# Sums of w_out 192 bytes further into their buffers, and the MLP's pool 192 bytes further

## The chip, the cores and the metric

The kernel runs on 1 core of one Trainium2 chip. The metric is the device time of one execution in microseconds (us); the kernel before takes 634.56 us, the median of 3 runs (634.4 to 636.4). Lower is better.

## The reference

Three layers follow one another on 8 batches of 576 rows, 4608 rows in all, in fp32.

```python
def _attn_ref(q, k, v, p):            # q, k, v [8, 8, 576, 64]; p [8, 8, 32, 64]
    p_packed = sm_attn(p, k, v)       # 32 packed rows per head attend over 576 keys
    return sm_attn(q, p_packed, p_packed)

def _moe_ref(x, phi, w1, w2):         # x [4608, 512], 8 experts of 4 slots, F 1024
    logits = x @ phi                  # [4608, 32]
    d = softmax(logits, axis=0); slot_input = d.T @ x        # [32, 512]
    slot_out[e] = np.maximum(slot_input[e] @ w1[e], 0.0) @ w2[e]
    c = softmax(logits, axis=1); return c @ slot_out          # [4608, 512]

def _moe2_ref(x, w_in, w_out):        # w_in [512, 2048], w_out [2048, 512]
    h = x @ w_in
    g = h * np.tanh(softplus(h))      # Mish
    return g @ w_out                  # [4608, 512]
```

## The kernel before, in words

The first two layers take the first 230 us or so. The rest is the third layer, the MLP, and only this part is touched. Since `c @ slot_out @ w_in` has rank 32, `slot_out @ w_in` is formed once (the tile MS), and the product with the combine weights (CS) gives `h` directly: four matmuls of 256 columns per step (L1205, `emit_h`). ScalarE applies Mish (L1210). The 4608 rows are cut into 18 blocks `n` of 256, the 2048 hidden features into 4 chunks `c` of 512. A step is one (n, c): it multiplies a 256 x 512 piece of g with a 512 x 512 piece of w_out and adds it into PSUM banks that hold the block's output.

To keep fp32 accuracy with one-pass matmuls of type fp32r, each operand is split into a high part that is exact in fp32r and a low rest: gh and gl (ScalarE casts, VectorE subtracts, `emit_c`), and whi and wlo for w_out. Each product is then three matmuls: high by high, high by low, low by high.

There are two kinds of steps. A plain step (the first blocks) multiplies with moving operands of 512 columns straight from whi and wlo (the tile W3, shown as W). A fast step (`fast`, 59 of 72) uses a scheme of Strassen's kind: the 2 x 2 blocks of g and of w_out are combined into sums, and 7 products of half size replace 8. The sums of g are S, with its parts Sh and Sl (k = 0 to 3; `emit_m`, `emit_c`), made anew in every step. The sums of w_out are T1, T2, T3 for each of the 4 chunks, made once in `build_t` and then only read. The order of the products of a fast step is in `emit_o`: Z (gh by W), V (S1 by T2), W (S2 by T3), X or W (S3 by W), U (S0 by T1), Y and X (gh by W). Each product is 6 matmuls of 256 columns (1024 bytes per partition): 4 with the high weights, 2 with the low ones. With two `h` matmuls after Z and two after the product into the bank W a fast step has 46 matmuls; in the last two steps, which have no `h` to prepare, 42. In the first fast step of a block the first matmul on bank W is 512 columns wide (`TT["open"]`) and clears both halves.

In a matmul g, S or MS is the stationary operand (weights, loaded before each matmul), W, T or CS the moving one. Where they lie in SBUF, in bytes from the start of a partition:

| buffer | role | address before | modulo 512 |
|---|---|---|---|
| whi, wlo (W3) | moving | 115712 + 2048 i, halves of 1024 | 0 |
| CS | moving (`h`) | 189440 + 1024 n | 0 |
| T, 7 buffers of ring_a | moving | 18240 + 4608 i, and + 1024 z f | 320 |
| T, 4 buffers of ring_x | moving | 66880 + 4608 i, and + 1024 z f | 320 |
| T, one in pool g2 (i == 11) | moving | 109888, and + 1024 z f | 320 |
| gh, gl (pool wg) | weights | 50496 + 4096 i, and + 512 f | 320 |
| S, Sh, Sl (pool g2) | weights (Sh, Sl) | 85312, 93504, 101696, two buffers of 4096 each | 320 |
| MS | weights (`h`) | 181248 + 512 m | 0 |

The pool g2 is opened when the pools of the conversion (t2, tp) are closed, at step N0, and lies where they lay. The order of all instructions is written by hand. TensorE runs through the steps without a gap as long as the sums and casts of the next step come in time; VectorE makes them and also empties the PSUM banks (`emit_store`, L1376).

Of the kernel before, what the change touches and what calls it, by code (L numbers as in the profile page):

```python
# [9 lines left out]
F32 = mybir.dt.float32  # L10
F32R = mybir.dt.float32r
# [8 lines left out]
def kernel(  # L20
# [1124 lines left out]
    def msb_c(n, copy, mp, i=0, w=512):  # L1145
        copy(out=msb[n][:, i:i + w], in_=mp[:, 0:w])

    def emit_mr(n, mr, i=0, w=512):
        nc.tensor.matmul(mr[:, 0:w], lhsT=idrep, rhs=msb[n][:, i:i + w], start=True, stop=True)

    def ms_c(n, mr, i=0, w=512):
        nc.scalar.copy(out=MS[:, 512 * n + i:512 * n + i + w], in_=mr[:, 0:w])

    def ms_l(n, mr, i=0, w=512):
        dst = MS[64:128, 512 * n + i:512 * n + i + w]
        nc.vector.tensor_tensor(out=dst, in0=mr[64:128, 0:w], in1=dst.bitcast(F32), op=ALU.subtract)
# [14 lines left out]
    def fast(n, c):  # L1171

        return not PLAIN.get(n, 0) >> c & 1
# [23 lines left out]
    def emit_h(n, c, z):  # L1197

        if not z:
            s = tp.tile([128, 1024], F32, name="s", tag="s") if steps.index((n, c)) < N0 else two_of("s")  # L1200
            blk["m", n, c] = s.rearrange("p (f n) -> p f n", f=4), None
        hp = ps_b.tile([128, 512], F32, name="h3", tag="h3", bufs=2)
        for f in range(2):
            ft = 4 * c + 2 * z + f
            nc.tensor.matmul(  # L1205
                hp[:, 256 * f:256 * f + 256], lhsT=MS[:, 128 * ft:128 * ft + 128], rhs=CS[:, 256 * n:256 * n + 256],
                start=True, stop=True,
            )
        s = blk["m", n, c][0][:, 2 * z:2 * z + 2]
        nc.scalar.activation(out=s, in_=hp.rearrange("p (f n) -> p f n", f=2), func=AF.Mish)  # L1210
# [36 lines left out]
    def wparts(c):  # L1247
        return whi[:, 4 * c:4 * c + 4], wlo[:, 4 * c:4 * c + 4]

    def build_t(c, ws=None):  # L1250

        H, L = wparts(c)
        TT[c] = []

        def alloc():
            for k in range(3):
                i = (3 * c + k + 9) % 12
                if i < 7:
                    t = ring_a.tile([128, 18 * D], F32, name="T", tag="ring%d" % (5, 6, 2, 0, 1, 4, 3)[i])
                elif i < 11:  # L1260
                    t = ring_x.tile([128, 18 * D], F32, name="T", tag=("kT", "qT")[i % 2])
                else:
                    t = g2.tile([128, 1280], F32, name="T", bufs=1)
                    TT["open"] = t.bitcast(F32R)[:, 256:1280].rearrange("p (z n) -> p z n", z=4)[:, 0:4:3]
                    nc.gpsimd.tensor_scalar_mul(
                        out=t[:, 1024:1280].bitcast(F32R).rearrange("p (z n) -> p z n", z=2),
                        in0=ident[:, None, :].to_broadcast([128, 2, 128]), scalar1=0.0,
                    )
                t = t[:, 0:1024].bitcast(F32R).rearrange("p (z f n) -> p z f n", z=2, f=2)
                TT[c].append((t[:, 0], t[:, 1]))  # L1270
            TT[c].append((H[:, 0:2, 256:512], L[:, 0:2, 256:512]))

        if c != 1:
            alloc()
        minus = lambda o, x, y: nc.vector.tensor_tensor(out=o, in0=x, in1=y, op=ALU.subtract)
        if ws is None:
            wa, wb = (w[:, 0:1024].rearrange("p (f n) -> p f n", f=2) for w in (held if c == 1 else (two_of("osb"), two_of("osb"))))
            B11, B12, B21, B22 = (w[:, :, 256 * j:256 * j + 256] for w in (wa, wb) for j in range(2))
            T4 = B21
            if c != 1:  # L1280
                for w, f in ((wa, 0), (wb, 2)):
                    nc.vector.tensor_tensor(out=w, in0=H[:, f:f + 2].bitcast(F32), in1=L[:, f:f + 2].bitcast(F32), op=ALU.add)
                yield
            minus(B11, B12, B11)
            minus(B12, B22, B12)
            minus(B22, B22, B11)
            minus(B21, B21, B22)
            T = B11, B22, B12
            yield
            if c == 1:  # L1290
                alloc()
            for (hi, lo), x in zip(TT[c], T):
                nc.scalar.copy(out=hi, in_=x)
            for (hi, lo), x in zip(TT[c], T):
                minus(lo, x, hi.bitcast(F32))
        else:
            T4 = AY[:, 4096:4608].rearrange("p (f n) -> p f n", f=2)
            for f in range(2):
                (B11, B12), (B21, B22) = ((w[:, 0:256], w[:, 256:512]) for w in (ws[f], ws[2 + f]))
                minus(B11, B12, B11)  # L1300
                minus(B12, B22, B12)
                minus(B22, B22, B11)
                minus(T4[:, f], B21, B22)
            yield
            fx = [(f, hi, lo, x) for f in range(2) for (hi, lo), x in zip(TT[c], (ws[f][:, 0:256], ws[2 + f][:, 256:512], ws[f][:, 256:512]))]
            for f, hi, lo, x in fx:
                nc.scalar.copy(out=hi[:, f], in_=x)
            for f, hi, lo, x in fx:
                minus(lo[:, f], x, hi[:, f].bitcast(F32))
        yield  # L1310
        hi, lo = TT[c][3]
        nc.scalar.copy(out=hi, in_=T4)
        minus(lo, T4, hi.bitcast(F32))
        yield
# [54 lines left out]
    def quads(n):  # L1369
        if ("q", n) not in blk:  # L1370
            osb = two_of("osb").rearrange("p (z n) -> p z n", z=2)
            blk["q", n] = [osb] + [osb[:, i, 256 * j:256 * j + 256] for i in range(2) for j in range(2)]
        return blk["q", n]
# [36 lines left out]
    def bank(x):  # L1410
        if x in "xs":
            return ps_x.tile([128, 512], F32, name="o3", tag="x") if x == "x" else ps_so.tile([128, 512], F32, name="so")
        return ps_b.tile([128, 512], F32, name="o3", tag=x, bufs=2 if x == "h3" else 1)
# [25 lines left out]
    def two_of(x):  # L1439

        turn[x] ^= 1
        i = (0 if x == "osb" else 2048) + 1024 * turn[x]
        return AY[:, i:i + 1024]
# [40 lines left out]
    for i, (n, c) in enumerate(steps):  # L1484
        if i == 2:
            R.update(X=bank("X2"), Y=bank("Y2"))
        if i == N0:
            wp.close()
            g2 = ctx.enter_context(tc.tile_pool(name="g2", bufs=2, reuse_waits="tile"))
        if i == N0 + 2:  # L1490
            R.update(Z=R["X0"], V=R["Y0"], W=R["X1"], U=R["Y1"])
        nx = steps[i + 2] if i + 2 < len(steps) else None
        last_s = fast(n, c) and c == ORDER[n][-1]

        def mid(z):
            if z == 0 and last_s:
                nc.scalar.copy(out=quads(n)[1], in_=rq("Z"))
            if z == 1 and last_s:
                add(quads(n)[2], quads(n)[1], rq("V"))
            if z in (0, 2) and nx:  # L1500
                emit_h(*nx, z // 2)
                if i == 0:
                    m = 2 + z // 2
                    blk["mr", m] = bank("XY"[z // 2] + "2")
                    emit_mr(m, blk["mr", m])

        if i + 1 < len(steps):
            emit_c(*steps[i + 1])
        if i == 0:
            msb_c(2, nc.scalar.copy, mp2)  # L1510
            msb_c(3, nc.scalar.copy, mp3)
            ms_c(1, mr1)
            ms_l(1, mr1)
        if i < N0:
            cvt(CVT[i][0])
        emit_o(n, c, mid)
        if i == 0:
            cvt("u4 m4")
            for m in (2, 3):
                ms_c(m, blk["mr", m])  # L1520
                ms_l(m, blk["mr", m])
        early = c == ORDER[n][-1] and n + 1 in PLAIN and not fast(n + 1, ORDER[n + 1][0])
        if early and last_s:
            emit_store(n)
        if nx:
            emit_m(*nx)
        if i < N0:
            cvt(CVT[i][1])
        if i == N0 - 1:
            work[3] = build_t(3, [late_w[k][3] for k in range(12, 16)])  # L1530
        if c == ORDER[n][-1] and not (early and last_s):
            emit_store(n)
        for x in TW.get(i, ""):
            next(work[int(x)])
# [31 lines left out]
```

## Time and profile before

| | |
|---|---|
| time, median of 3 runs | 634.56 us (634.4 to 636.4) |
| profiled execution, its own time | 633.09 us |
| span of the profiled execution | 631.3 us |
| TensorE busy | 603.5 us, 96%, 5874 matmuls |
| VectorE busy | 499.5 us, 79% |
| ScalarE busy | 339.4 us, 54% |
| granted TensorE clock | full in all 40 slices |
| fast steps | 59, from about 290 us to the end |

A matmul's record begins when it is handed on and ends when its last column is out; several are under way at once. So busy time says little about the rate: what a matmul costs in a run of matmuls is the distance from one start to the next. Where the timeline merges matmuls into one row (x4, x2), the distance is the difference of the starts of two rows divided by the matmuls between them. Starts are printed to 0.01 us, so a distance over 12 matmuls is good to about 1 ns, one over 2 matmuls to about 5 ns.

### The profile page before, as it was taken

The page shows a single profiled execution, that of the slowest core. Times are in us where ns is not written, and L with a number is a line of the kernel's source. Part 1 is how long each engine was busy: PE and PEld are TensorE (multiplying, and loading weights), DVE is VectorE, ACT ScalarE, POOL GpSimd, SP SyncE. Part 2 cuts the span into 40 slices and gives each one's busy share as a digit, 9 for nine tenths or more (in the row PEclk, how much of TensorE's full clock was granted, in tenths as well). Part 3 has the DMA queues.
Part 4 walks back from the last instruction along what each step waited for, and adds up shares of the span by engine and source line. Part 5 has one row for each costly group of instructions (what it writes and reads, how often), then busy time and mean ns, then how long its engine had stood idle before and what let it go on. Part 6 is the DMA issues. An engine that isn't in the chain of part 4 may idle for free.

```text
span 631.3 us, 14397 instructions
## 1 busy us (share of the span) xinstructions
PE 603.5 (96%) x5874; PEld 522.3 (83%) x5874; DVE 499.5 (79%) x1004; ACT 339.4 (54%) x684; POOL 47.3 (7%) x73
## 2 busy tenths in 40 slices
PE   7799999998998999999999999999999999999997
PEld 4577777786434468888989999999999999999997
DVE  4998888978464388988999887788778877887883
ACT  3354555546334486665556555555555555555551
POOL 5122222112030000000000000000000000000000
PEclk9999999999999999999999999999999999999999
DMA  8998963999999962002110110011011101110100
GB/s 274 329 323 293 330 210 128 404 412 407 394 410 413 413 243 67 2 0 68 35 35 0 35 35 12 24 34 34 2 34 34 34 2 34 34 34 2 34 34 35
DMA packets 42162, 89.61 MB, mean 142 GB/s; under 512 B 10736, under 2 KB 19056, under 8 KB 42096
## 3 DMA queue, kind: packets, MB, share of 16 engines
q1 hardware_dynamic: 41696, 88.36, 39.2%
q8 instruction: 46, 0.75, 0.5%
q10 hardware_dynamic: 144, 0.26, 0.1%
q14 instruction: 20, 0.16, 0.1%
q0 software_dynamic: 256, 0.07, 0.1%
HBM read 79.23 MB, written 9.44 MB: 140 GB/s over the span
## 4 chain that ended last, share of the span: by engine, by line
PE 65%; DVE 19%; DMA 8%; ACT 5%; issue 2%; SPq 1%; DVEq 0%; POOL 0%; ACTq 0%; POOLq 0%
PE o L1327 44%; PE so L1327 7%; DMA AW<-in_moe_w_dram 6%; PE h L1205 5%; DVE kT L338 4%; DVE S L1221 2%; DVE A L510 1%; DVE AY L1376 1%; DVE mx L509 1%; PE s L490 1%; DVE Sl L1240 1%; DVE sm L525 1%; DMA AW<-in_q_dram 1%; DVE nmx L386 1%; DMA AC<-in_k_dram 1%
## 5 line engine op out<-in xcount | busy, mean ns | idle before, releaser
L1327 PE MATMUL o<-W,gh 128*128 128x256 f32 (+1 forms) x648 | 119.2, 311 | 0.5 <-DVE AY L1376 0.5
L1327 PE MATMUL o<-T,Sh 128*128 128x256 f32 x708 | 114.8, 284 | 1.0 <-DVE AY L1376 0.9
L1236 ACT CAST gh<-AY 128x512 fp32r<-128x512 f32 x118 | 54.7, 511 | 113.5 <-PE o L1327 113.5
L1327 PEld LDWEIGHTS o<-W,gh 128*128 128x128 f32 x648 | 95.6, 188 | 7.9 <-issue 1.3
L1327 PEld LDWEIGHTS o<-T,Sh 128*128 128x128 f32 x708 | 97.0, 189 | 2.1 <-issue 0.6
L1210 ACT ACTIVATE AY<-h 128x512 f32<-128x512 f32 x126 | 74.0, 594 | 26.3 <-PE h L1205 25.0
L1239 DVE TENSOR_TENSOR gl<-AY,gh 128x512 fp32r<-128x512 f32 x118 | 60.4, 553 | 33.3 <-ACT gh L1236 33.3
L1240 DVE TENSOR_TENSOR Sl<-S,Sh 128x1024 fp32r<-128x1024 f32 x59 | 72.1, 1223 | 9.2 <-ACT Sh L1237 9.2
L1327 PE MATMUL o<-T,Sl 128*128 128x256 f32 x354 | 71.2, 282 | 0.0
L1327 PE MATMUL o<-W,gl 128*128 128x256 f32 (+1 forms) x324 | 70.0, 308 | 0.0
L1237 ACT CAST Sh<-S 128x1024 fp32r<-128x1024 f32 x59 | 61.9, 1049 | 6.8 <-DVE S L1221 6.8
L1205 PE MATMUL h<-CS,W 128*128 128x256 f32 x288 | 56.2, 284 | 0.0
L1327 PEld LDWEIGHTS o<-W,gl 128*128 128x128 f32 x324 | 52.1, 188 | 4.0
L1327 PEld LDWEIGHTS o<-T,Sl 128*128 128x128 f32 x354 | 54.8, 190 | 0.0
L1221 DVE TENSOR_TENSOR S<-AY 128x256 f32<-128x256 f32 x118 | 49.6, 420 | 6.0 <-ACT AY L1210 6.0
L1376 DVE TENSOR_TENSOR AY<-AY,o 128x256 f32<-128x256 f32 x115 | 45.1, 417 | 9.1 <-PE o L1327 5.3
L1205 PEld LDWEIGHTS h<-CS,W 128*128 128x128 f32 x288 | 44.1, 188 | 3.1 <-ACT s L1210 0.8
L1327 PE MATMUL so<-W,gh 128*128 128x256 f32 (+1 forms) x268 | 45.4, 292 | 0.0
L1327 PEld LDWEIGHTS so<-W,gh 128*128 128x128 f32 x268 | 37.3, 188 | 2.4 <-ACT W L1191 0.3
L376 PE MATMUL s<-kT,win 128*128 128x288 f32 x128 | 34.7, 414 | 4.7 <-ACT win L388 3.8
L1327 PE MATMUL o<-W,Sh 128*128 128x256 f32 x236 | 37.5, 281 | 0.0
L490 PE MATMUL s<-win,qT 128*128 128x128 f32 x256 | 32.1, 278 | 1.8 <-ACT win L356 1.8
(263 smaller groups left out, 988.9 us busy)
## 6 DMA issues: line engine op xcount, KB each, us to landing
AW<-in_moe_w_dram SPq DMA_DIRECT2D x45, 512.0 KB, 10.1
r_wo<-in_moe_w_out_dram SPq DMA_DIRECT2D x16, 512.0 KB, 8.9
out_dram<-AY SPq DMA_DIRECT2D x64, 128.0 KB, 2.1
r_wi<-in_moe_w_in_dram SPq DMA_DIRECT2D x13, 512.0 KB, 10.5
AW<-in_q_dram SPq DMA_DIRECT2D x11, 576.0 KB, 5.3
AW<-in_k_dram SPq DMA_DIRECT2D x9, 576.0 KB, 7.3
AW<-in_v_dram SPq DMA_DIRECT2D x40, 128.0 KB, 5.0
AC<-in_moe_w_dram SPq DMA_DIRECT2D x10, 512.0 KB, 10.0
```

What stands on the lines that cost most here:

```text
L338: nc.vector.transpose(out=T[:, dh, main].rearrange("p (i r a) -> p a i r" if nm == "k" else "p (i a r) -> p a i r", i=4, a=4,), in_=x[:, 0 ...
L376: nc.tensor.matmul(ps[:, n, 0:288], lhsT=pBD[b % 2][:, hq, dh], rhs=kT[:, dh, 288 * n:288 * n + 288], start=(dh == 0), stop=(dh == 1),)
L490: nc.tensor.matmul(ps[:, k - lo], lhsT=d["qT", hq][:, dh, 64 + 128 * i:192 + 128 * i], rhs=ppBD[b % 2][:, hq, dh], start=(dh == 0), stop=( ...
L1205: nc.tensor.matmul(hp[:, 256 * f:256 * f + 256], lhsT=MS[:, 128 * ft:128 * ft + 128], rhs=CS[:, 256 * n:256 * n + 256], start=True, stop=True,
L1210: nc.scalar.activation(out=s, in_=hp.rearrange("p (f n) -> p f n", f=2), func=AF.Mish)
L1221: nc.vector.tensor_tensor(out=S[:, k], in0=x, in1=y, op=op)
L1236: nc.scalar.copy(out=gh[:, f, t], in_=s[:, f, t])
L1237: nc.scalar.copy(out=Sh, in_=S)
L1239: nc.vector.tensor_tensor(out=gl[:, f, t], in0=s[:, f, t], in1=gh[:, f, t].bitcast(F32), op=ALU.subtract)
L1240: nc.vector.tensor_tensor(out=Sl, in0=S, in1=Sh.bitcast(F32), op=ALU.subtract)
L1327: nc.tensor.matmul(o, lhsT=lhsT, rhs=rhs, start=first, stop=stop)
L1376: add = lambda o, x, y: nc.vector.tensor_tensor(out=o, in0=x, in1=y, op=ALU.add)
```

## The change

Each sum T of w_out begins 48 elements (192 bytes) further into its buffer of 4608 bytes; it takes 4096 of them, so it fits. The one T that lies in pool g2 keeps its place in its tile, but in g2 an unused tile of 192 bytes is allocated first, which moves everything in that pool by 192 bytes: S, Sh, Sl and that T.

```diff
@@ build_t, alloc @@
-                t = t[:, 0:1024].bitcast(F32R).rearrange("p (z f n) -> p z f n", z=2, f=2)
+                o = 0 if i == 11 else 48
+                t = t[:, o:o + 1024].bitcast(F32R).rearrange("p (z f n) -> p z f n", z=2, f=2)
@@ the loop over steps @@
         if i == N0:
             wp.close()
             g2 = ctx.enter_context(tc.tile_pool(name="g2", bufs=2, reuse_waits="tile"))
+            g2.tile([128, 48], F32, name="pad", bufs=1)
```

After it T begins at 0 modulo 512, and so do the weights Sh and Sl; gh and gl stay at 320. All instructions are the same, in the same order on every engine. One wait is new: the first S of the program now overlaps a buffer of the conversion pool that VectorE read last, so its first instruction waits for VectorE's own earlier work too. On VectorE, before (the names are the program's: S the sums of g, gl the low part of g, w a converted block of w_out):

```order
439 L1275 TENSOR_TENSOR T<-w_3413,T 128x256 [waits Activation_49]
440 L1275 TENSOR_TENSOR T<-w_3363,T 128x256 [waits Activation_49]
441 L1230 TENSOR_TENSOR gl<-AY,gh 128x1024 [waits PE_49,Activation_49]
442 L1221 TENSOR_TENSOR S<-AY 128x256 [waits Activation_49]
443 L1221 TENSOR_TENSOR S<-S,AY 128x256 [waits DVE_49]
```

And after, at the same place:

```order
439 L1276 TENSOR_TENSOR T<-w_3413,T 128x256 [waits Activation_49]
440 L1276 TENSOR_TENSOR T<-w_3363,T 128x256 [waits Activation_49]
441 L1230 TENSOR_TENSOR gl<-AY,gh 128x1024 [waits PE_49,Activation_49]
442 L1221 TENSOR_TENSOR S<-AY 128x256 [waits DVE_49,Activation_49]
443 L1221 TENSOR_TENSOR S<-S,AY 128x256 [waits DVE_49]
```

Nothing moved; the fourth row has the second wait.

## Rows read from the trace of the kernel before

**Rows 1.** The page's parts 1 and 2: engines, then 40 slices of the span.
```profile
PE 603.5 (96%) x5874; PEld 522.3 (83%) x5874; DVE 499.5 (79%) x1004; ACT 339.4 (54%) x684; POOL 47.3 (7%) x73
...
PEclk9999999999999999999999999999999999999999
```

**Rows 2.** The page's part 4: chain that ended last, by engine, then by line.
```profile
PE 65%; DVE 19%; DMA 8%; ACT 5%; issue 2%; SPq 1%; DVEq 0%; POOL 0%; ACTq 0%; POOLq 0%
PE o L1327 44%; PE so L1327 7%; DMA AW<-in_moe_w_dram 6%; PE h L1205 5%; DVE kT L338 4%; DVE S L1221 2%; DVE A L510 1%; DVE AY L1376 1%; DVE mx L509 1%; PE s L490 1%; DVE Sl L1240 1%; DVE sm L525 1%; DMA AW<-in_q_dram 1%; DVE nmx L386 1%; DMA AC<-in_k_dram 1%
```

**Rows 3.** Waits of TensorE, 312 to 631 us (total us, times, longest us).
```profile
PE o L1327 <- DVE AY L1376: 1.1, 3, 0.4
```

**Rows 4.** Timeline of TensorE, end of the last but one step, last step (start, length).
```profile
621.27 0.62 PE L1327 MATMUL o<-W,gh 128*128 128x256 f32 x4
...
622.63 0.63 PE L1327 MATMUL o<-T,Sh 128*128 128x256 f32 x4
...
623.34 0.64 PE L1327 MATMUL o<-T,Sh 128*128 128x256 f32 x4
623.81 0.40 PE L1327 MATMUL o<-T,Sl 128*128 128x256 f32 x2
624.05 0.64 PE L1327 MATMUL o<-W,Sh 128*128 128x256 f32 x4
624.52 0.39 PE L1327 MATMUL o<-W,Sl 128*128 128x256 f32 x2
624.75 0.63 PE L1327 MATMUL o<-T,Sh 128*128 128x256 f32 x4
...
625.46 0.63 PE L1327 MATMUL o<-W,gh 128*128 128x256 f32 x4
```

**Rows 5.** Timeline of TensorE in plain steps, 512 columns wide.
```profile
242.34 0.62 PE L1205 MATMUL h<-CS,W 128*128 128x256 f32 x4
242.81 2.03 PE L1327 MATMUL o<-W,gh 128*128 128x512 f32 x8
...
245.60 2.03 PE L1327 MATMUL so<-W,gh 128*128 128x512 f32 x8
...
248.40 0.62 PE L1205 MATMUL h<-CS,W 128*128 128x256 f32 x4
```

**Rows 6.** Timeline of one whole fast step, 481.92 to 487.31 us, TensorE's and VectorE's rows.
```profile
481.92 0.62 PE L1327 MATMUL so<-W,gh 128*128 128x256 f32 x4
...
482.60 0.40 PE L1205 MATMUL h<-CS,W 128*128 128x256 f32 x2
482.60 1.03 DVE L1239 TENSOR_TENSOR gl<-AY,gh 128x512 fp32r<-128x512 f32 x2 [0.53 <-ACT gh L1236]
...
482.84 0.64 PE L1327 MATMUL o<-T,Sh 128*128 128x256 f32 x4
...
484.27 0.40 PE L1205 MATMUL h<-CS,W 128*128 128x256 f32 x2
484.51 0.64 PE L1327 MATMUL o<-W,Sh 128*128 128x256 f32 x4
...
485.22 0.64 PE L1327 MATMUL o<-T,Sh 128*128 128x256 f32 x4
...
485.93 0.64 PE L1327 MATMUL o<-W,gh 128*128 128x256 f32 x4
...
486.63 0.62 PE L1327 MATMUL o<-W,gh 128*128 128x256 f32 x4
...
487.31 0.28 PE L1327 MATMUL so<-W,gh 128*128 128x256 f32 x1
```

**Rows 7.** The page's part 5, T's groups (count, busy us, mean ns of one).
```profile
L1327 PE MATMUL o<-T,Sh 128*128 128x256 f32 x708 | 114.8, 284 | 1.0 <-DVE AY L1376 0.9
...
L1327 PE MATMUL o<-T,Sl 128*128 128x256 f32 x354 | 71.2, 282 | 0.0
```

**Rows 8.** Busy time from 312 us on: length, PE, PEld, DVE, ACT, POOL, PEclk, DMA.
```profile
312.00:631.30 319.30, 313.74 (x2639) 311.16 (x2637) 257.23 (x515) 175.22 (x304) 0.00 (x0) 1.00 0.10 26
```

## The prediction

> **What bounds the kernel now.** I read the page's engine line first: TensorE is busy 96% of the span, VectorE 79%, and the granted clock is full in every slice [rows 1], the higher of the two levels, 2.4 GHz. Then the chain of waits: 51% of the span runs through the MLP's products at L1327 and 5% through `h` at L1205 [rows 2]; nothing else there belongs to the stretch of the fast steps in any amount. Then the waits of TensorE over 319 us of fast steps: 1.1 us in all [rows 3]. So in that stretch TensorE is fed without gaps, and the time is the number of matmuls times the distance from one start to the next. The timeline gives that distance, and it is not the same for all of them, though all have 256 columns:
>
> - Moving operand W, weights gh and gl, in the last two steps: from 621.27 to 622.63 us there are 12 matmuls, 1.36 us, **113.3 ns** each [rows 4].
> - Moving operand T: from 622.63 to 624.05 12 matmuls, 1.42 us, 118.3 ns; the two at the end of that run, 623.81 to 624.05, **120 ns** each [rows 4]. In a step in the middle 482.84 to 484.27, 12 in 1.43 us, 119.2 ns [rows 6].
> - Moving operand W with 512 columns: 242.81 to 248.40 without four `h` at the end holds 24 matmuls, 5.59 us, **232.9 ns** each [rows 5].
>
> 256 columns at 2.4 GHz are 106.7 ns, 512 are 213.3. What is left over is 6.6 ns, 13.3 ns and 19.6 ns, that is 1 : 2 : 3. Now count the multiples of 512 bytes that lie inside the operand. A run of 1024 bytes that begins at one has 1; a run of 1024 bytes that begins at 320 modulo 512 (T) has 2; a run of 2048 bytes that begins at one has 3. The three distances fit one rule without a free term: columns at full rate plus about 6.7 ns for every multiple of 512 bytes that the moving operand crosses. Multiples of 256 or of 1024 bytes don't fit (for W, T and the wide ones the counts would be 3 : 4 : 7 and 0 : 1 : 1). That the cause is T and not its weights shows in the last step: W with the weights Sh and Sl, the same buffers as for T, starts at 117.5 ns (624.05 to 624.52, 4 matmuls) and falls to 115 ns in its last two (624.52 to 624.75) [rows 4]. Each run seems to carry the rate of the one before into its first two or three matmuls.
>
> **What the skill has on it.** The Trainium skill, "TensorE: Matmul & The Clock Gate", section "Back-to-back issue gap", gives columns divided by 2.4 plus a fixed 2.5 ns, with no term for the address; an estimate by it is 109.2 ns for W and T alike and 215.8 ns for 512 columns. The rows differ: what is left over is not fixed but grows from 6.6 to 19.6 ns. The Trainium skill, "SBUF — State Buffer", section "Specifications (TRN2)", has lines of 16 bytes, and by that 320 would be as good a start as 0, since both begin a line; the change would then do nothing. Here the measured distances decide for a dependence on something coarser, as far as they go: no row shows a T at another place.
>
> **The change, part by part.** It removes and adds no instruction, and the order stays.
>
> 1. T, 18 matmuls in each of 59 fast steps (708 with Sh and 354 with Sl, 1062 = 59 x 18 [rows 7]). Now 1.43 us for the two products V and W and 0.71 us for U (485.22 to 485.93), 2.14 us a step [rows 6]. At 113.3 ns: 2.04 us. Gain 0.10 us a step.
> 2. The six matmuls of Y that follow T inherit its rate: 485.93 to 486.63, 0.70 us [rows 6], against 6 x 113.3 ns = 0.68. Gain 0.02 us a step.
> 3. S3 by W, 6 matmuls, 484.51 to 485.22, 0.71 us; `h`, 2 + 2 matmuls, 482.60 to 482.84 and 484.27 to 484.51, 0.24 us each, 120 ns a matmul [rows 6]. Their moving operands already begin at a multiple of 512 and do not move. If all their surplus came from the T around them, they would give 0.03 + 0.03 us a step; if it has another cause (the first two `h` come right after a run at 113.3 and are slow at once, and VectorE's gl begins at the same 482.60), nothing. I take nothing for the sum and keep 0.06 us for the range.
> 4. The other way round: if what makes `h` slow beside VectorE's work holds V and W back as well, their 12 matmuls fall only to the 117.5 ns of W with Sh, 1.41 us, a gain of 0.02, and only U (0.03) and Y (0.02) gain in full: 0.07 us a step, the low end.
> 5. Weights Sh and Sl now begin at 0 instead of 320 modulo 512. No row shows Sh there. The nearest are `h`, with weights and moving operand both at 0: 120 ns in the fast step [rows 6] and, among plain steps, 242.34 to 242.81, 4 in 0.47 us, 117.5 ns [rows 5]. gh at 320 with W at 0 runs at 113.3. So between no loss and 6.7 ns on 24 matmuls a step. For the forecast I take no loss, because S at 320 in the middle step is as slow as `h` at 0; the loss is a rival below.
> 6. VectorE and ScalarE read and write S, Sh, Sl and T at other addresses. The same operation on W, at 0, and on gl, at 320, are both plain subtractions; I cost this at nothing. VectorE is busy 257.2 of 319.3 us there, ScalarE 175.2 [rows 8]: 81% and 55%. With steps 2 to 3% shorter VectorE comes to 83 or 84%, and casts and sums are made for the step after next; it does not become late. If it did, its waits would show on TensorE, where they now are 1.1 us in all [rows 3].
> 7. The one new wait is on VectorE's first S, for VectorE's own work on T, with a whole gl between (the same subtraction, in two pieces, takes 1.03 us at 482.60 [rows 6]). It has been done by then, so I take nothing. At most it is that 1.03 us, once; behind it stand the other sums S of that step, which the step after needs.
>
> The sum: 0.12 us x 59 = 7.1 us. The profiled execution took 633.09 us, with a span of 631.3; it becomes 626.0. It took 1.47 us less than the median of the runs, so the forecast for the median is 634.56 - 7.1 = **627.5 us**. Its own range goes from 0.07 x 59 = 4.1 us (630.4) to 0.18 x 59 = 10.6 us (623.9), where all 46 matmuls run at 113.3 ns: 5.39 - 5.21 = 0.18 us a step.
>
> **The rivals.**
>
> *The start does not matter.* T is slow for what else is common to all T: T and its weights both lie below address 115712 of SBUF, while W lies above it and W's weights below. For it: `h` is slow although its moving operand begins at a multiple of 512, and there moving operand and weights both lie above. This is also where the 16-byte lines of the Trainium skill, "SBUF — State Buffer", would lead. Against it: it does not give the 1 : 2 : 3 of the three distances, for W lies in one place whether 256 or 512 of its columns are read. Then nothing changes: 634.5 us, 633.5 to 635.5.
>
> *The same start modulo 512 in both operands is what costs (slower).* Before, T and its weights are both at 320 and slow, `h` and its weights both at 0 and slow, W at 0 with weights at 320 fast. After the change T, and now S3 by W too, are at 0 with weights at 0. T stays at 120 ns and the six of S3 by W go from 118.3 to 120 or worse. With 24 matmuls at 120: 2.88 us against 2.14 + 0.71 = 2.85, 0.03 us a step, 1.8 us: 636.4. The upper price is that of `h` taken as a difference: from the first matmul after Z to the first of Y the step with four `h` takes 485.93 - 482.60 = 3.33 us [rows 6], the one without 625.46 - 622.63 = 2.83 us [rows 4], so each `h` costs 125 ns. 24 x 125 ns = 3.00: 0.15 us a step, 8.9 us: 643.4. It decides as soon as T stays above 119 ns. Against it: the four `h` of plain steps, with the same starts, come in at 117.5 rather than 120, and 512 columns fit only the first rule.
>
> **How the numbers follow.** Forecast 57%, start does not matter 28%, same start costs 15%. A change of under 0.3% (1.9 us) cannot be told from none here. The forecast's low end of 4.1 us is outside that, the second rival inside, the third mostly outside above: faster 58%, same 28%, slower 14%. The range that should hold 8 in 10 takes the forecast's own and the whole of "no change": 624.0 to 636.2; the rest lies mostly above. The likeliest case by itself: 623.9 to 630.4.
>
> **What would show it.** In the profile after, the distance of T in the last step: 12 matmuls in 1.36 us instead of 1.42. If so, step 1 is right; if they take 1.42 to 1.44, one of the rivals, and then the six of W with Sh decide: 0.70 as now (start does not matter) or 0.72 and more (same start costs). The distance of a whole fast step, now 5.39 us, gives the sum: 5.27 in the forecast. `h` and S3 by W at 113 or at 118 to 120 settle step 3. If TensorE's waits rise above a few us, step 6 is wrong. The prediction is wrong if T falls to 113 ns and the time does not follow, or if T stays.

## The result, and the profile after

The change makes the kernel slower: 638.58 us, the median of 4 runs (637.86 to 639.66), against 634.55 us before, a ratio of 1.0058 with a 95% interval of 1.0033 to 1.0083. Here and below a ratio is that of the means, against runs of the kernel before taken beside it (their medians: 633.57 to 634.55 us). The forecast was 627.5 us. The profiled execution took 638.09 us with a span of 636.3.

The page after, engines, clock and chain of waits, with T's two groups (count, busy us, mean ns of one), answers to [rows 1, 2, 7]:

```profile
PE 610.4 (96%) x5874; PEld 528.3 (83%) x5874; DVE 500.5 (79%) x1004; ACT 339.4 (53%) x684; POOL 47.9 (8%) x73
...
PEclk9899999999999999999999999999999999999999
...
PE 74%; DVE 15%; DMA 4%; ACT 4%; issue 1%; SPq 0%; DVEq 0%; POOL 0%; ACTq 0%; POOLq 0%
...
L1328 PE MATMUL o<-T,Sh 128*128 128x256 f32 x708 | 115.7, 285 | 0.6 <-DVE AY L1377 0.6
...
L1328 PE MATMUL o<-T,Sl 128*128 128x256 f32 x354 | 71.2, 283 | 0.0
```

TensorE is as full as it was, the clock is at its higher level throughout the MLP, VectorE and ScalarE do the same work in nearly the same time. T's busy time rises by 0.9 us and says nothing of the distances: a mean record of 285 ns covers several matmuls under way at once. The waits of TensorE from 312 us on, then the same stretch as busy times:

```profile
PE o L1328 <- DVE AY L1377: 0.8, 3, 0.4
```

```profile
312.00:636.30 324.30, 319.19 (x2638) 316.62 (x2636) 257.90 (x514) 175.18 (x303) 0.00 (x0) 1.00 0.09 26
```

Waits fell from 1.1 to 0.8 us [rows 3]; VectorE has 0.7 us more than in [rows 8], in a stretch 5 us longer. So TensorE hardly waits, and yet the stretch is longer. The first matmul of T starts at 295.0 us before and at 294.8 after, the last matmul of the MLP ends at 627.0 and at 632.0: the whole 5 us lie in the fast steps, and they are the distance from one start to the next. The timeline of TensorE, last two steps, against [rows 4]:

```profile
625.45 0.63 PE L1328 MATMUL o<-W,gh 128*128 128x256 f32 x4
...
626.86 0.64 PE L1328 MATMUL so<-W,gh 128*128 128x256 f32 x4
...
627.57 0.64 PE L1328 MATMUL o<-T,Sh 128*128 128x256 f32 x4
...
629.01 0.64 PE L1328 MATMUL o<-W,Sh 128*128 128x256 f32 x4
...
629.73 0.64 PE L1328 MATMUL o<-T,Sh 128*128 128x256 f32 x4
...
630.45 0.63 PE L1328 MATMUL o<-W,gh 128*128 128x256 f32 x4
```

T, 627.57 to 629.01, 12 matmuls in 1.44 us: 120 ns, where 113 was forecast. W with Sh, 0.72 us for six: 120 ns, up from 117. And W with gh, 625.45 to 627.57, 18 matmuls in 2.12 us: 117.8 ns, where it was 113.3. Neither W nor gh has moved. From 625.30 to 627.77 us VectorE and ScalarE are idle, so the 117.8 ns isn't their doing. A whole fast step in the middle, against [rows 6]:

```profile
484.22 0.64 PE L1328 MATMUL so<-W,gh 128*128 128x256 f32 x4
...
484.93 0.40 PE L1205 MATMUL h<-CS,W 128*128 128x256 f32 x2
485.17 0.64 PE L1328 MATMUL o<-T,Sh 128*128 128x256 f32 x4
...
486.85 0.64 PE L1328 MATMUL o<-W,Sh 128*128 128x256 f32 x4
...
488.29 0.63 PE L1328 MATMUL o<-W,gh 128*128 128x256 f32 x4
...
489.70 0.64 PE L1328 MATMUL so<-W,gh 128*128 128x256 f32 x4
```

484.22 to 489.70 is 5.48 us, against 5.39. By product, from the starts of all matmuls of the last 43 steps with `h` (mean distance from a start to the next, ns; 32 steps without the 512-wide opening matmul, then the mean length of those steps and of the 11 with it; the experiments below stand in the same table; 115.6 is the mean of two rates, see there):

```
                        Z      h     V,W     S     U    Y,X   | step  step with opening
before                113.3  118.5  119.3  118.2 118.8  114.9 | 5387   5467
after                 118.1  119.8  120.0  120.0 119.6  117.8 | 5478   5592
T moved alone         118.2  118.8  118.0  117.8 117.8  117.8 | 5427   5540
S moved alone         113.4  121.1  118.1  119.6 118.2  114.3 | 5380   5493
CS moved alone        113.3  119.0  118.9  117.2 120.3  115.5 | 5393   5507
MS moved alone        113.3  117.3  118.4  113.9 117.8  114.4 | 5333   5447
T and CS moved        113.3  120.8  114.3  115.3 113.3  113.3 | 5267   5387
T and MS moved        115.6  115.6  115.6  115.6 115.6  115.6 | 5213 or 5418
the same but one T    113.3  113.3  113.3  113.3 113.3  113.3 | 5213   5373
```

Z, V and so on are the products as the code names them; Z, Y and X are gh and gl by W, S is S3 by W, and V, W, U have T. Of the 91 ns that a step loses, 29 are Z's (six matmuls) and 35 those of Y and X (twelve), together some two thirds, and none of their operands has moved.

### The profile page after: what moved, and what is told of

Its sections match the earlier page's. It is cut to its first block, busy times and chain, and to the rows that moved or that the text cites. A ratio compares the mean times of both kernels' runs of the same rounds, so it can differ in the third digit from the quotient of the medians.

```text
span 636.3 us, 14398 instructions
## 1 busy us (share of the span) xinstructions
PE 610.4 (96%) x5874; PEld 528.3 (83%) x5874; DVE 500.5 (79%) x1004; ACT 339.4 (53%) x684; POOL 47.9 (8%) x73
## 4 chain that ended last, share of the span: by engine, by line
PE 74%; DVE 15%; DMA 4%; ACT 4%; issue 1%; SPq 0%; DVEq 0%; POOL 0%; ACTq 0%; POOLq 0%
PE o L1328 48%; PE so L1328 8%; PE h L1205 5%; DVE kT L338 4%; PE hp L989 2%; DMA AW<-in_moe_w_dram 2%; PE so L1016 1%; DVE A L510 1%; DVE mx L509 1%; PE s L490 1%; DMA AC<-in_moe_w_dram 1%; DVE AY L1377 1%; DVE nmx L386 1%; DMA AC<-in_q_dram 1%; ACT AT L548 1%
## 5 line engine op out<-in xcount | busy, mean ns | idle before, releaser
L1328 PE MATMUL o<-W,gh 128*128 128x256 f32 (+1 forms) x648 | 120.3, 313 | 0.5 <-DVE AY L1377 0.5
L1328 PEld LDWEIGHTS o<-T,Sh 128*128 128x128 f32 x708 | 98.6, 192 | 1.7 <-DVE AY L1377 0.6
```

Source lines behind the costliest of these rows:

```text
L1328: nc.tensor.matmul(o, lhsT=lhsT, rhs=rhs, start=first, stop=stop)
```

## The experiments

After the result three explanations were open: that the place or the buffer counts and not the start; that T's start and S's start each have a price of their own; and that what counts is how far the weights' start stands from the moving operand's, with something that lasts beyond the single matmul. "Start" is below always the address in the partition, and a pair 0|320 has its moving operand at 0 and its weights at 320 modulo 512.

**T alone.** All twelve T to 0, S left at 320, so T stands like W by gh, 0|320.

```diff
-                    t = g2.tile([128, 1280], F32, name="T", bufs=1)
+                    t = g2.tile([128, 1328], F32, name="T", bufs=1)
...
-                t = t[:, 0:1024].bitcast(F32R).rearrange("p (z f n) -> p z f n", z=2, f=2)
+                t = t[:, 48:48 + 1024].bitcast(F32R).rearrange("p (z f n) -> p z f n", z=2, f=2)
```

> All twelve T begin at 0 modulo 512, the weights Sh and Sl stay at 320 (no pad). Theory P (the pair: a matmul is slow, 120 ns, when the moving operand and the weights that are loaded meanwhile begin at the same place modulo 512, and fast, 113.3 ns, when not): T by Sh is now 0 with 320 like W by gh, so T falls to 113.3 to 115 ns, S3 by W and gh by W run at 113.3; only the four h (0 with 0) stay near 118. The step falls from 5.39 to 5.23 to 5.28 us, the time to 626 to 629 us. Theory Q (two costs by themselves: a moving operand off a multiple of 512 costs 6.7 ns, weights on a multiple of 512 cost 6.7 ns): the same here, 626 to 629 us. Theory R (the place in SBUF decides, not the start): T stays at 119 to 120 ns, the time at 634 to 635 us.

Measured: 636.62 us (636.01 to 637.25), ratio 1.0041 (1.0023 to 1.0058). Slower; theories P and Q (626 to 629) both missed. The timeline of TensorE, one step:

```profile
603.82 0.63 PE L1327 MATMUL so<-W,gh 128*128 128x256 f32 x4
...
604.52 0.40 PE L1205 MATMUL h<-CS,W 128*128 128x256 f32 x2
604.76 0.63 PE L1327 MATMUL o<-T,Sh 128*128 128x256 f32 x4
...
607.83 0.64 PE L1327 MATMUL o<-W,gh 128*128 128x256 f32 x4
...
609.24 0.63 PE L1327 MATMUL so<-W,gh 128*128 128x256 f32 x4
```

T is a little quicker than before (118.0 and 117.8 ns), not at 113.3, and W by gh slower: 607.83 to 609.24 is 12 in 1.41 us, 117.5 ns. All products lie between 117.8 and 118.2 ns. So T by itself would have been the better half of the change, if the other products had kept their rate.

**S alone.** The unused tile stays, T stays at 320.

```diff
-                    t = g2.tile([128, 1280], F32, name="T", bufs=1)
+                    t = g2.tile([128, 1360], F32, name="T", bufs=1)[:, 80:1360]
...
+            g2.tile([128, 48], F32, name="pad", bufs=1)
```

> S, Sh and Sl moved by the pad to 0 modulo 512, all twelve T left at 320. Theory P: T by Sh is 320 with 0, fast, 113.3 to 115 ns; S3 by W becomes 0 with 0, 120 ns; the step falls by 0.10 and gains 0.02, 5.30 us, the time is 629 to 631 us. Theory Q: T pays twice, 127 ns, and S3 by W pays once, 120: the step rises by 18 x 7.5 + 6 x 2 = 0.15 us, 643 us. Theory R: 634 to 635 us for T, and if it is the weights' place at 0 that made the changed kernel slow, 638 us.

Measured: 634.3 us (632.89 to 637.51), ratio 1.0003 (0.9984 to 1.0023): the same. P (629 to 631) and Q (643) missed; R's time came, but not its reason, since T changed with the start of its weights alone. T now has 320|0 and runs near 118, S3 by W has 0|0 and runs near 120, and gh by W is back at 113.3. Neither half adds up to the whole with the other by fixed prices: T alone +2.1 us, S alone 0, both +4.0, and gh by W is slow in two of the three.

**A table of starts.** The kernel before, followed by runs of 24 matmuls that do no part of the computation, with the starts of both operands in steps of 64 bytes and in different regions of SBUF; VectorE reads the result between two runs.

> The kernel before, with matmuls of fp32r added at its end while all other engines rest: 24 in a row for each of 8 starts of the moving operand (0, 64, ... 448 modulo 512) by 8 starts of the weights, both in the tile W3; then four pairs of starts (0 or 320) with the moving operand or the weights or both in the low buffers of T; four pairs at 512 columns; and two runs that go from a fast pair through a pair of equal starts back to the fast pair. Its time is that of the kernel before plus some 230 us and says nothing. Theory P: 120 ns on the diagonal of the table (equal starts), 113.3 ns away from it, perhaps a band around the diagonal, and the same in all places. Theory Q: 113.3 where the moving operand is at 0 and the weights are not, 120 with one of the costs, 127 with both; the diagonal is nothing special. Theory R: the table is flat, and the place (low or high) makes the difference between 113.3 and 120 ns. In the last two runs, if the rate of the fast pair depends on what came before, the 48 matmuls after the equal pair stay above 113.3 ns for more than 3 of them; if not, they are back at 113.3 after 3.

Measured in the timeline of TensorE, the first moving start, weights at 128, 192, 256, 320:

```profile
634.92 3.11 PE L1555 MATMUL probe<-W 128*128 128x256 f32 x24 [0.27 <-DVE AY L1558]
638.29 3.09 PE L1555 MATMUL probe<-W 128*128 128x256 f32 x24 [0.27 <-DVE AY L1558]
641.65 3.14 PE L1555 MATMUL probe<-W 128*128 128x256 f32 x24 [0.27 <-DVE AY L1558]
645.05 3.00 PE L1555 MATMUL probe<-W 128*128 128x256 f32 x24 [0.27 <-DVE AY L1558]
```

Weights at 256 take 3.14 us, at 320 3.00, with the same moving operand. From the starts, mean distance of the last 15 of each run, ns (four of the eight rows, four of the eight columns; the others repeat with 256, but for the cell named below):

```
moving \ weights     0      64     128     192
      0            120.0  113.3  118.7  117.8
     64            117.8  120.0  113.3  118.7
    128            118.7  117.7  119.9  113.3
    192            117.8  118.7  117.8  119.8
```

What counts is the difference, weights minus moving operand, modulo 256: 0 gives 120.0, 64 (the good difference, below) gives 113.3, 128 gives 118.7, 192 gives 117.8. One cell of the 64 does not fit: 192|0 has the good difference and ran at 117.8, while 192|256, 448|0 and 448|256 ran at 113.3. So the difference alone does not settle the rate. With one or both operands in other buffers below address 115712 the four corner pairs give the same: 0|0 119.9 to 120.0, 0|320 113.3, 320|0 117.8, 320|320 119.9 to 120.0. That the place counts is out. And a memory showed: 24 at 0|320, then 24 at 0|0, then 48 at 0|320 stayed at 117.7 to the end; with 320|320 in the middle they were back at 113.3 after four.

**T and CS.** T as above, and CS 192 bytes further, so that `h` is 192|0: every pair of the step at a difference of 64.

```diff
-    CS = arena.tile([128, NT], F32R, name="CS", tag="AC")
+    CS = arena.tile([128, NT + 48], F32R, name="CS", tag="AC")[:, 48:]
```

> All T at 0 modulo 512 as in the run with T alone, S left at 320, and CS, the moving operand of h, 192 bytes further (h: moving at 192, weights at 0). Theory D (what the table shows: the rate depends on the distance weights minus moving operand modulo 256; 64 is the best, 113.3 ns, 0 the worst, 120; and a stretch at distance 64 stays at 117.7 after a stretch at distance 0 that it was entered from by a move of the weights): here every matmul of a fast step is at distance 64 and nothing spoils it. All 46 at 113.3 ns, 5.21 us a step, 10 us less than before: 624 to 626 us. Theory H (the distance counts, but without memory; VectorE's and ScalarE's work is what held the fast steps of the T-alone kernel at 117.7): the step stays at 5.40 us, 635 to 637 us.

Measured: 628.23 us (627.41 to 631.15), ratio 0.9916 (0.988 to 0.9952): faster, though not down to the 624 to 626 expected. The timeline of TensorE, one step:

```profile
607.07 0.62 PE L1327 MATMUL so<-W,gh 128*128 128x256 f32 x4
...
607.75 0.41 PE L1205 MATMUL h<-CS,W 128*128 128x256 f32 x2
607.99 0.63 PE L1327 MATMUL o<-T,Sh 128*128 128x256 f32 x4
...
609.36 0.41 PE L1205 MATMUL h<-CS,W 128*128 128x256 f32 x2
...
612.34 0.62 PE L1327 MATMUL so<-W,gh 128*128 128x256 f32 x4
```

607.99 to 609.36 is 12 of T in 1.37 us, 114.2 ns, and the step 5.27 us. In the table above all products are at or near 113.3 but `h` (120.8) and the matmuls right behind it: there the moving start goes from 0 to 192 and back, and a neighbour at another start seems to cost for some matmuls even where each pair is a good one. For `h` itself this is not separated from its pair, 192|0, the one good pair that the table above has at 117.8. That the twelve matmuls of V and W lose most of their surplus only when `h`, 4 matmuls in 46, moves as well is the plainest sight of the memory.

**CS alone.**

> The kernel before with CS alone moved by 192 bytes: h at distance 64, T by Sh still at distance 0. Theory D: T stays at 120 and S3 by W and gh by W at 113.3 to 115 as in the last step of the kernel before, h at 113 to 115 where they follow gh by W, at the rate of T where they stand between T; a step of 46 comes to 18 x 118.3 + 28 x 114 = 5.32 us, 0.07 less than before, 4 us: 630 to 631. Theory H: h stays at 118 to 120, the time at 634 to 635.

Measured: 634.56 us (632.9 to 639.36), ratio 1.0012 (0.9987 to 1.0036): no gain, and the expectation missed. `h`, now at a good difference, with T at 320|320 on one side and W on the other, is at 119.0. Per step V, W and S3 by W gain some 11 ns, and U, Y and X lose some 16.

**Finer steps, and what brings the rate back.** Differences in steps of 16 bytes, 512 columns, and runs of 24 at one pair followed by 40 at a good one.

> The kernel before with matmuls added at its end, all with moving operand and weights in W3: the distance weights minus moving operand from 0 to 240 bytes in steps of 16 at 256 columns; from 0 to 448 in steps of 64 at 512 columns; and nine runs of 24 matmuls of one pair followed without a pause by 40 of another. Its time says nothing. Theory D: a period of 256 bytes, 0 the worst, 64 near the best, smooth or in steps between; at 512 columns a period of 256 too, with 0 better (227 to 230) than 64 (233.5). Of the nine: pairs at distance 0 with moving operand at 0, left for a pair at distance 64 by moving the weights, stay at 117.7; left by moving the moving operand, they come back to 113.3; the same with 320 in both. Theory H: all nine are back at 113.3 after 3 matmuls; but two such runs already were not.

Measured: of the 16 differences only 64 gives 113.3; the others lie between 116.8 and 120.3. With 512 columns difference 0 is the best, 226.7, and the others 228.9 to 233.3 (the last 12 of each run). So 0|320, the good one for 256 columns, is the worst for the wide ones (233.3). Of the histories, 0|0 before 0|320 leaves 117.8, and 0|0 before 448|0 leaves 113.3. Left by a new start of the weights the slow rate stayed in five runs of six, left by a new start of the moving operand it went in three of three. The exception is 0|192 before 0|320: back at 113.3, with the moving operand where it was. (The last run below shows another.)

**T and MS, MS alone.** `h` to 0|64 by moving its weights: then every pair has the good difference and no neighbour has another moving start (modulo 256). The room comes from an arena that was 64 elements larger than it needs to be. The cut shows MS's part; T's part is that of T alone, and the run with MS alone is without it.

```diff
-    AW, AC, AY = (arena.tile([128, n], F32, name=x, tag=x) for x, n in (("AW", 1024 * RW), ("AC", 1024 * RC), ("AY", 4856)))
+    AW, AC, AY = (arena.tile([128, n], F32, name=x, tag=x) for x, n in (("AW", 1024 * RW + 64), ("AC", 1024 * RC), ("AY", 4792)))
...
-    MS = W3[:, 2 * FT * DM:]
+    MS = W3[:, 2 * FT * DM + 16:]
```

> All twelve T begin at 0 modulo 256 bytes, S, Sh, Sl, gh and gl stay where they are (64 modulo 256), and MS begins 64 bytes further (64 modulo 256) while CS stays at 0. So the weights of every matmul of a step stand 64 bytes behind its moving operand, modulo 256, and a moving operand starts at the same place in every product, so no two neighbours are crossed either. The theory of the distance with a memory (D): nothing sets the slow state, all 46 matmuls of a fast step start 113.3 ns apart, 5.21 us a step instead of 5.39; 59 x 0.176 = 10.4 us less than before: about 624 us, some 3 to 4 us below the kernel with T and CS moved. The rival that h is slow since VectorE and ScalarE work beside it: h stays at 118 to 123 ns and the six behind it at 114 to 118, as in the kernel with T and CS moved, about 628 us. The rival that only moving operands count (a start of T at 320 or not): as the kernel with T alone moved, 636 us.

Measured: 630.47 us (629.3 to 632.25), ratio 0.9934 (0.991 to 0.9958), 4.1 us of the 10.4 expected. The timeline of TensorE shows why: a step at one rate, then the matmul of 512 columns, and another rate.

```profile
491.09 0.62 PE L1327 MATMUL so<-W,gh 128*128 128x256 f32 x4
...
496.30 0.62 PE L1327 MATMUL so<-W,gh 128*128 128x256 f32 x4
...
497.89 0.74 PE L1327 MATMUL o<-T,Sh 128*128 128x512 f32 x4
...
498.94 0.63 PE L1327 MATMUL o<-W,Sh 128*128 128x256 f32 x4
499.41 0.40 PE L1327 MATMUL o<-W,Sl 128*128 128x256 f32 x2
499.65 0.63 PE L1327 MATMUL o<-T,Sh 128*128 128x256 f32 x4
500.12 0.40 PE L1327 MATMUL o<-T,Sl 128*128 128x256 f32 x2
500.35 0.64 PE L1327 MATMUL o<-W,gh 128*128 128x256 f32 x4
```

491.09 to 496.30 is 46 matmuls in 5.21 us, 113.3 ns each. Behind the wide one, 498.94 to 500.35, 12 matmuls take 1.41 us, 117.5. At the next block's wide matmul it goes back, and so at each of the 11 blocks from 390 us on: the steps between are all 5.213 or all 5.418 us. (At the block before, 368 us, it stayed slow.) The good difference has two rates that keep themselves up.

> Only MS begins 64 bytes further; T stays at 320 modulo 512 with its weights at 320, as before. Theory D (distance with a memory): h, 4 of 46, now stands at the good distance. T (18 of 46) stands at distance 0 and runs at 119 to 120 ns; what follows it with a moving operand that starts elsewhere recovers over about five matmuls. So g stays at 113.3, h falls from 120 to between 113 and 118, since T lies right before and behind it: at best 4 x 6.7 ns = 0.03 us a step and 1.6 us in all, 633 to 634.5 us. If it is h that makes T slow (T would run at 113 were it not for h), T falls too and the time goes below 630 us.

Measured: 631.63 us (629.96 to 634.84), ratio 0.9956 (0.9939 to 0.9974), better than expected: `h` itself gains little (118.5 to 117.3), but the six of S3 by W behind it fall from 118.2 to 113.9. This fits the histories above: from T to `h` the moving start changes, and no 0|0 is left to spoil what follows.

**T and MS, but one T in its old place.** The T in pool g2, which the wide matmul reads, stays at 320|320. Its six matmuls cost more, but the start of the moving operand changes in front of them and behind. Against the kernel with T and MS moved (that T's smaller tile is left out of the cut):

```diff
-                t = t[:, 48:48 + 1024].bitcast(F32R).rearrange("p (z f n) -> p z f n", z=2, f=2)
+                o = 0 if i == 11 else 48
+                t = t[:, o:o + 1024].bitcast(F32R).rearrange("p (z f n) -> p z f n", z=2, f=2)
```

> As the kernel with T and MS moved, but the T that lies in pool g2 keeps its place (320 modulo 512): its six matmuls in one step of four stand at distance 0 again and begin elsewhere than their neighbours. In the kernel with T and MS moved every step ran at exactly one of two rates, 113.3 ns a matmul (5.213 us) or 117.7 ns (5.418 us), and it changed from one to the other at the one matmul of 512 columns that each block of four steps has; with all distances at 64, nothing brought it back. The theory of the distance with a memory (D, in the form that a change of the moving operand's start brings the fast state back): the six at 320 cost 6 to 7 ns each and the way out some 20 ns, about 0.06 us in 15 steps, and after each of them the state is fast again; the other steps take 5.21 us all. 59 x 0.173 - 15 x 0.06 = 9.3 us less than before: 625 to 626 us. Rival: the slow steps of the kernel with T and MS moved have a cause outside the starts (a DMA, VectorE's work): half the steps stay at 5.42, 630 us.

Measured: 628.08 us (625.06 to 630.92), ratio 0.9906 (0.9872 to 0.994). Of the last 43 steps all 32 without the opening matmul take 5.213 or 5.214 us, 113.3 ns a matmul; those with it 5.373. The rival, half of the steps at 5.42, is out. The timeline of TensorE around one such opening matmul:

```profile
602.72 0.75 PE L1328 MATMUL o<-T,Sh 128*128 128x512 f32 x4
...
603.54 0.40 PE L1205 MATMUL h<-CS,W 128*128 128x256 f32 x2
603.78 0.62 PE L1328 MATMUL o<-W,Sh 128*128 128x256 f32 x4
...
604.46 0.62 PE L1328 MATMUL o<-T,Sh 128*128 128x256 f32 x4
...
605.14 0.62 PE L1328 MATMUL o<-W,gh 128*128 128x256 f32 x4
```

Behind it the six of S3 by W take 0.68 us, and the rate is back. The MLP from its first product to its end took 393.4 us here, 395.8 with T and CS moved, 401.5 before and 406.8 after. Of the 8.1 us against before, where 9.3 were expected, the last 43 steps give 6.6 (32 x 0.174 + 11 x 0.094); the earlier ones, which partly wait for T to be made (TensorE's waits from 312 us on are 2.1 us, 1.0 more than before), give less than their share. The time in front of the MLP was 228.0 us in this execution and 225.5 in that of before; with T and MS moved, whose first two layers are the same as here, it was 225.4. Such differences widen the spread of the runs; the medians show 5.5 us. The medians don't tell this version from the one with T and CS moved; both beat the kernel before.

**What flips the rate.** The kernel before with runs of 12 good matmuls (0|320), a few others, 20 good ones.

> The kernel before with matmuls appended that do no part of the computation: 12 matmuls of 256 columns at the good distance (moving operand at 0, weights at 320 modulo 512), then some others (X), then 20 at the good distance again. X is 1, 2 or 3 of 512 columns, 1 or 2 of 512 columns in two pieces, 1 or 2 of 128 columns, one of 64, 1, 2, 3, 4 or 8 with both at 0, 1 or 2 with both at 320, and 512 columns at distance 0. Then the same after a run at 0|0 that leaves 117.7 ns behind. If the state is a phase between the streams of moving operands and of weights that each matmul at the wrong distance or of another length shifts, then one of 512 columns leaves 117.7 behind it, and two of them may bring 113.3 back; how many at 0|0 are needed is seen in the rows with 1 to 8. If the state is one of memory for a place (a start that weights had), matmuls of 512 or 128 columns with the same starts change nothing, all rows with X at 0|320 stay at 113.3, and only those with 0|0 leave 117.7.

Measured, distances from start to start worked out from the trace (ns, the first after the pause left out where it is the pause's; "then" begins with the first of the 20):

```
before              in between                 then
114 113 113 ...     1 of 512                   118 118 117 118 118 ... to the end
113 113 114 ...     2 of 512 (227 236)         118 113 114 113 113 ...
118 117 119 ...     3 of 512 (233 233 234)     121 116 114 114 113 ...
118 118 117 ...     1 of 512 (231)             116 113 114 114 113 ...
118 118 117 ...     2 of 512 (231 228)         120 117 118 117 118 ...
113 113 114 ...     1 of 64                    200 117 118 118 118 ...
113 113 114 ...     2 at 0|0                   118 118 117 119 117 ... and so after 3, 4, 8
113 113 114 ...     1 at 320|320               118 124 119 113 113 ...
114 113 113 ...     2 at 320|320               116 118 117 119 117 ...
```

In all seven runs with them each matmul of 512 columns at 0|320 turns the rate over, in either direction; an even number leaves it as it was (in two pieces, as the opening matmul has them, the same). So the memory is not of a start that weights had, since these have the same starts as the others. In the kernels it is no rule: with T and CS moved the opening matmul, 0|320, made a fast rate slow at all 11 blocks from 390 us on, but with T alone moved it is 0|320 too, and the rate was slow before and behind it at all 11. The timeline of TensorE with T alone moved:

```profile
610.89 0.75 PE L1327 MATMUL o<-T,Sh 128*128 128x512 f32 x4
...
611.96 0.63 PE L1327 MATMUL o<-W,Sh 128*128 128x256 f32 x4
...
613.37 0.64 PE L1327 MATMUL o<-W,gh 128*128 128x256 f32 x4
```

611.96 to 613.37 is 12 in 1.41 us, 117.5 ns. Two, three, four or eight of 256 columns at 0|0 leave the slow rate (the runs with one began slow). One or two of 512 columns at 0|0 made a slow rate fast in three runs of three, and one at 320|320 left it slow. Of the 18 runs that begin with 12 at the good difference these settled at 113.3 in 12 and at 117.7 in 6. It isn't all a count of two: one matmul of 128 columns left the slow rate slow in one run and made it fast in another. What decides it stays open.

## Why the prediction was wrong

*What bounds the kernel* held: hardly a wait (0.8 to 2.1 us from 312 us on), and the time is the number of matmuls times the distance between starts, in each of the nine kernels. One reading did not hold: VectorE's S, Sl and AY in the chain [rows 2] do belong to the fast steps. From 290 to 350 us of before they have 41% of the chain and TensorE 23%, so a distance saved in those first steps need not be time saved, and the 59 steps do not count alike.

*The rule of the multiples of 512 bytes* is what failed, and step 1 with it. It rested on three distances in the proportion 1 : 2 : 3, and the difference of the two starts orders them instead. T ran at 118 to 120 because it stood at 320|320, a difference of 0, not because of the boundaries in its 1024 bytes: in the table 320|384, which crosses as many, is at 113.3. The wide ones ran at 233 because they had the difference 64: with 0|0 they cross as many multiples and take 226.7. W with Sh against T with Sh, which the forecast read as showing that T is the cause and not its weights, compared 0|320 with 320|320 and could not tell the two apart. Three numbers and one free choice of modulus were too little for a rule.

*Step 1*, T to 113.3 ns, failed at 120.0: the change moved T's weights by the same 192 bytes, and the difference stayed 0. The forecast had the reason as its last rival (same start in both operands) at 15%, with its condition, T above 119 ns. Its modulus was off, 256 and not 512, which makes no difference for T here.

*Step 2*, Y inherits T's rate, was right as a mechanism and too small: not two or three matmuls inherit, but all that follow until something turns the rate over. Z goes from 113.3 to 118.1 and Y and X from 114.9 to 117.8, 64 of the 91 ns lost per step.

*Step 3* left open whether `h` and S3 by W are slow by themselves. `h` is: it was 0|0. S3 by W, 0|320, is not: with MS alone moved it ran at 113.9, so before it was slow by what `h` left behind. VectorE's gl, which the forecast suspected beside `h`, is not it: in the last row of the table `h` runs at 113.3 beside the same gl. In before `h` spoils what follows, and it seems to be the way from T at 320|320 to W at 0, the very thing that the change takes away, that brought gh by W back to 113.3: with S alone moved T still began at 320 and gh by W came back, with T alone moved it did not.

*Step 5* took no loss for Sh and Sl at 0, because S3 by W at 320 was as slow as `h` at 0; that was the slowness that `h` left behind. S3 by W went from 0|320 to 0|0, 118.2 to 120.0 ns, 11 ns a step. With T's own 13 ns and 5 for `h` this is about the rest of the 91. The last rival's low price, 1.8 us, had only such terms; its high one, 8.9 us, was taken from `h`, and the 4.0 us lie between. "The start does not matter" was wrong too, and its condition, six of W with Sh at 0.70 us, did not come: 0.72.

*Steps 6 and 7*, VectorE and the new wait at nothing, held: TensorE's waits from 312 us on are 0.8 us, and T begins 0.2 us earlier than before.

The plain steps, for which the forecast had no term, did not change: 242.60 to 248.20, 24 wide matmuls in 5.60 us, 233.3 ns, against [rows 5].

```profile
242.14 0.62 PE L1205 MATMUL h<-CS,W 128*128 128x256 f32 x4
242.60 2.03 PE L1328 MATMUL o<-W,gh 128*128 128x512 f32 x8
...
248.20 0.39 PE L1205 MATMUL h<-CS,W 128*128 128x256 f32 x2
```

Their 233.3 could be 226.7 with gh, gl at the starts of W; that was not tried in the kernel.

## What to carry to other kernels

Where matmuls of equal length follow one another without waits, look at the distance from start to start, not at busy time, and list for each the start of its weights minus that of its moving operand: moving one operand alone, or both by the same amount, are different changes. Four matmuls of 46 can set the rate of others (V and W at 118.0 or 114.3 ns, as `h` stands), so a change that is tried on one product must be judged by the products that it does not touch. A proportion that fits three numbers is a reason to measure a fourth, not yet a rule.

## What was not expected of the hardware

- With 256 columns of fp32r the distance between starts depends on weights' start minus moving operand's start modulo 256 bytes: 113.3 ns at 64 (in 15 of the table's 16 cells; 117.8 in one), 120.0 at 0, 117.8 and 118.7 at 192 and 128, and between 116.8 and 120.3 at other multiples of 16. With 512 columns it is 226.7 at 0 and up to 233.3. Whether the weights in use count or those loaded meanwhile no run separates.
- At the good difference two rates keep themselves up, 113.3 and 117.7 ns, and a matmul of another length or difference can turn one into the other; one of 512 columns at that difference did so in all seven runs of the probe that had it and at 11 of 12 blocks of the kernel with T and MS moved, but at none of 11 with T alone moved. What decides it stays open.
- The Trainium skill, "SBUF — State Buffer", section "Who interferes with whom", gives TensorE two independent read ports, one for the moving operand and one for the weights, and says that PE never waits on anyone. The table of starts does not fit that as far as these two reads go: the same matmuls take 113.3 or 120.0 ns by nothing but the starts of the two. What in the chip they meet in, no run here shows.
